# Five plain feature groups instead of six ahead of the block products, and more token tiles transposed by DMA

## The chip, the cores and the metric

The kernel runs on one core of a Trainium2 chip. The metric is the device time of one execution in microseconds (us); three executions of the kernel before gave a median of 938.21 us (937.78 to 938.38).

## What is computed

Two kinds of layer alternate, A, B, A, B, each added to its input after a layer norm over the 1024 features of each of 2048 tokens. Layer A is a spectral filter; layer B, which the change touches, is a two-matrix network with the Mish activation. Everything is bf16 at the borders.

```
def _A_ref(x, w_r, w_i):                       # x: 1 x 2048 x 1024
    X = rfft2(x.astype(float32), axes=(-2, -1))
    return irfft2(X * (w_r + 1j * w_i), s=(2048, 1024)).astype(bfloat16)

def _B_ref(x, w1, b1, w2):                     # w1: 1024 x 3584, w2: 3584 x 1024
    h = x @ w1 + b1
    sp = log1p(exp(-abs(h))) + where(h > 0, h, 0)
    return (h * tanh(sp)) @ w2

x = A_x
x = x + _A_ref(_layernorm(x), A_w_r, A_w_i)
x = x + _B_ref(_layernorm(x), B_w1, B_b1, B_w2)
x = x + _A_ref(_layernorm(x), A_w_r, A_w_i)
x = x + _B_ref(_layernorm(x), B_w1, B_b1, B_w2)
```

## The kernel before, in words

**Order.** The program is written out by hand: every call adds an instruction to the in-order program of one engine (PE, DVE, ACT, POOL, or SP, which only issues DMAs), and the waits follow from the buffers that the instruction reads and writes. So the order of the Python calls is the order on each engine, and an instruction that waits holds up everything behind it on its engine. SBUF is one arena that is handed out by offset (`alloc`); a buffer inherits the waits of whatever lay there before.

**Tokens and features in layer B** (`layer_B`, L1085; it is called twice, the second time with `last=True`). The 2048 tokens are 16 tiles of 128, and 4 tiles make a chunk, so chunks 0 and 1 are the first half (tiles 0 to 7), chunks 2 and 3 the second. The 3584 features are 14 groups (`fg`) of 256. A tile is normalised on DVE (`apply`, L517) and then transposed into the chunk's buffer `XT[c]`. There are two ways: `transposed` (L1100) does 8 transposes on PE (L1109) and copies the PSUM bank out on DVE or ACT (L1114); `turned` (L1119) prepares 8 DMA transposes of 128x128 on SP's queue, which `turn(n)` (L1130) issues n at a time. `normal(j)` (L1461) is `apply` followed by `turned`.

**First half, first matrix.** The first groups are computed plainly by `mm1` (L1134): per chunk and group two outputs of 8 matmuls each, 512 tokens wide, or 256 wide where only half of the chunk is there yet; the Mish runs on ACT (L1152). Weights come into `w1_buf`, which layer A fills at its end (L950). Calls given as `mid` come between the two outputs. The remaining groups go through `quads` (L1178): one group for both chunks together, as a Strassen-like product with 7 block products of 4 matmuls (28 in all, L1186) where the plain way takes 32. It needs sums of the weight blocks and of the token blocks (`token_sums`, L1156). An iteration n of `quads` has this order on PE: A11 and S2 of group n, then A22 and S4 of group n-1, then S1, A12 and S3 of group n. After S4 of group n-1 the function `after(n-1)` is called, which places the work of other engines.

**Weight slots.** A slot of 7168 bytes a partition holds 4096 bytes of raw weights and three sums. `fill_slot` (L1071) works in two ways. The first time a group is met, in the first layer B, SP loads the raw weights (512 KB), POOL makes four sums (L1081), and POOL's queue stores the slot to a scratch tensor (896 KB). Afterwards SP loads the finished slot (896 KB) from scratch. Each block product waits for the whole slot, sums included (L1188). There are four slots WE0 to WE3 and three slots WS0 to WS2, which lie where `w1_buf` lay. In the kernel before, `quads` runs groups 6 to 13: seven have a slot of their own, and group 13 refills WE0 in `after(0)`, to be used in iteration 7.

**Second matrix and second half.** `products` (L1276) multiplies the activations of the first half by the second matrix in 7 stages of 4 token tiles, 14 matmuls each (L1268). `extra(n, t)` (L1535) is called after every one of these 28 steps: it calls `turn(2)`, so that the transposes still waiting go out two a step. At step (1, 3) it makes the scales of tiles 12 to 15, hands tile 12 to the DMA transposes and normalises 13, 14 and 15, which PE transposes at step (2, 2); ACT copies these out. Then `quads` runs all 14 groups for the second half, and `products` ends the layer. There the three slots WS0 to WS2 are used in turn, each refilled in `after(n)` for group n+3.

The lines that the steps of the prediction touch, as they stand before:

```
        mm1(0, 4)
        at_tiles(1)
        mm1(0, 5, mid=turns(1, 0, 1))
...
            if n > 3:
                normal(4 + n)
                turn(4)
...
                    reads=[s.res, s.rs] + list(res), writes=[self.r_bank[bank]])
```

`turns(1, 0, 1)` are the PE transposes of tiles 4 and 5; `stats_dve`, `scales` and `apply` for these two tiles come on DVE after the residual additions of tiles 4 to 7 (L1396).

Of the kernel before, what the change touches and what calls it, by code (L numbers as in the profile page):

```python
# [180 lines left out]
class KB:  # L181
# [513 lines left out]
    def layer_A(self, li):  # L695
# [6 lines left out]
        o, K = self.o, 1024  # L702
# [244 lines left out]
        self.residual_first()  # L947
        if li == 0:
            self.op(self.pool, lambda e: e.tensor_copy(self.B1[:], self.B1h[:]), reads=[self.r_b1h], writes=[self.r_b1])
        self.w1_buf = [self.alloc(f"W1_{i}", (self.ob["WS"] + i * 4096, 140 * K)[i > 4], [8, 256]) for i in range(6)]  # L950
        for fg in range(6):
            self.load_w1(self.w1_buf[fg].ap, fg, [self.w1_buf[fg].res], after=self.r_ut)

    @staticmethod
# [130 lines left out]
    def layer_B(self, li, last):  # L1085
# [7 lines left out]
        def open_xt(c):  # L1093
            off = self.ob[f"XT{c}"]
            XT[c] = self.alloc(f"XT{c}", off, [8, 512])
            r_xt[c] = self.sub_res(XT[c], f"xt{c}h", 2, off, 8192)
            for r in r_xt[c]:
                r.begin()

        def transposed(c, t, xn, eng=None, bank=None):  # L1100
            if bank is None:
                bank = 6 + nt[0] % 2
                nt[0] += 1
            xn.unread = False
            if t == 0:
                open_xt(c)
            fns = []
            for db in range(8):
                fns.append(lambda e, db=db: e.transpose(PSb[:, bank, db * P:(db + 1) * P], xn.ap[:, db * P:(db + 1) * P],  # L1109
                                                        self.IDENT[:]))  # L1110
            self.group(fns, reads=[xn.res, self.r_ident], writes=[self.r_bank[bank]])
            dst = XT[c].ap[:, :, t * P:(t + 1) * P]
            src = PSb[:, bank, :].rearrange("p (a b) -> p a b", b=P)
            fn = (lambda e: e.activation(dst, src, ACT.Copy)) if eng is act else (lambda e: e.tensor_copy(dst, src))  # L1114
            self.op(eng or dve, fn, reads=[self.r_bank[bank]], parts=[r_xt[c][t // 2]])
# [3 lines left out]
        def turned(c, t, xn):  # L1119

            x, r = XT[c], r_xt[c][t // 2]
            for db in range(8):
                def one(db=db):
                    self.dma(sp, x.ap[:, db, t * P:(t + 1) * P], xn.ap[:, db * P:(db + 1) * P], f"xt{c}_{t}", reads=[xn.res],
                             parts=[r], transpose=True)
                    if db == 7:
                        xn.unread = False
                turning.append(one)
# [5 lines left out]
        def mm1(c, fg, half=None, mid=()):  # L1134
            wb = self.w1_buf[fg]
            x = XT[c]
            tok = slice(0, 512) if half is None else slice(256 * half, 256 * half + 256)
            w = tok.stop - tok.start
            for fl in range(2):
                if fl:  # L1140
                    for f in mid:
                        f()
                ft = 2 * fg + fl
                bank = nh[0] % 3
                nh[0] += 1
                fns = []
                for db in range(8):
                    fns.append(lambda e, db=db, bank=bank, fl=fl: e.matmul(  # L1148
                        PS[:, bank, 0:w], wb.ap[:, db, fl * P:(fl + 1) * P], x.ap[:, db, tok], start=(db == 0), stop=(db == 7)))
                self.group(fns, reads=[wb.res] + (r_xt[c] if half is None else [r_xt[c][half]]), writes=[self.r_bank[bank]])  # L1150
                at, ra = at_of(c, ft), r_at[c % 2][ft]
                self.op(act, lambda e, bank=bank, ft=ft, at=at: e.activation(at[:, tok], PS[:, bank, 0:w], ACT.Mish,  # L1152
                                                                      bias=self.B1[:, ft:ft + 1]),
                        reads=[self.r_bank[bank], self.r_b1], writes=[ra])
# [99 lines left out]
        def load_b(stages, n, k):  # L1254
            PB[n][k] = load_w2(stages[n][1], k, f"R{(2 * n + k + 1) % 4}")
# [122 lines left out]
        def at_tiles(c):  # L1378
            r_at[c] = [None] * NF
            for k in range(2):  # L1380
                off = self.ob["A"] + 14336 * (2 * k + c)
                AT[c][k] = b = self.alloc(f"AT{c}{k}", off, [NF // 2, 512])
                for i in range(NF // 2):
                    r = r_at[c][2 * i + k] = Res(f"AT{c}_{2 * i + k}")
                    r.inherit(b.res)
                    self.live.append((off + i * 1024, off + i * 1024 + 1024, r))
# [12 lines left out]
        def turns(c, *ts):  # L1399
            return [lambda t=t: transposed(c, t, xn[4 * c + t]) for t in ts]  # L1400
# [40 lines left out]
        for fg in range(1, 4):  # L1441
            mm1(0, fg, 1)
            if fg > 1:
                self.stats_act(4 + fg)
        mm1(0, 4)
        at_tiles(1)
        mm1(0, 5, mid=turns(1, 0, 1))
        self.sums_to_mv(6, 2)
        self.scales(6, 2)
        for j in (6, 7):  # L1450
# [1 line left out]
        gate = Res("gate")  # L1452
        gate.set_w(dve, dve.count)
        early = self.open_slots("WE", self.ob["W2"], 0, 1, 2, 3)
        for n in range(4):
            self.fill_slot(early[n], 6 + n, [gate])
        for fg in range(2):
            mm1(1, fg, 0, mid=turns(1, 2, 3) if fg else ())
        for fg in range(2):
            mm1(1, fg, 1)  # L1460
        def normal(j):  # L1461
            if j % 4 == 0:
                open_xt(j // 4)
            turned(j // 4, j % 4, self.apply(j))

        ws = []
        for fg in range(2, 6):
            if fg in (2, 4, 5):
                ws += self.open_slots("WS", self.ob["WS"], len(ws))
                self.fill_slot(ws[-1], 9 + len(ws))  # L1470
            mm1(1, fg)
            if fg == 2:
                token_sums(0, last=False)
            if fg == 3:
                for j in range(8, 12):
                    residual(j)
        order = early + ws + early[:1]
        B = token_sums(0)
        self.xn_buf = self.xn_out + [self.alloc(f"XN{i}", self.ob["XN2"] + i * 2048, [self.D]) for i in range(2)]

        def after(n):
            if n == 0:
                self.fill_slot(order[7], 13)
            if 1 <= n < 4:
                load_b(STD, n // 3, (n - 1) % 2)
            if n < 4:
                self.stats_dve(8 + n)
            if n == 4:
                self.scales(8, 4)
            if n > 3:  # L1490
                normal(4 + n)
                turn(4)
            for j in ((), (), (), (), (), (12, 13), (14,), (15,))[n]:
                residual(j)
        quads(list(range(6, 14)), order, B, after, lead)
        self.junk = self.alloc("JUNK2", self.ob["JUNK2"], [self.D])
        self.xn_buf = [self.alloc(f"XN{i}", self.ob["XN12"] + i * 2048, [self.D]) for i in range(2)] + self.xn_out
        w2 = {}
        if not last:
            for name, k, slot, prog in (("B21", 1, "R0", sp), ("B12", 0, "Q1", sp), ("B22", 0, "Q3", pool), ("B12", 1, "Q2", pool),  # L1500
                                        ("B22", 1, "Q4", sp)):
                w2[slot] = load_w2(name, k, slot, prog)
            PB[1][1] = w2["R0"]
        else:
            load_b(STD, 1, 1)
            self.fill_slot(ws[2], 2)
# [28 lines left out]
        def extra(n, t):  # L1535
            if n == 0:
                self.stats_act(12 + t)
            if not last:
                own_sums(n, t)
            if (n, t) == (1, 3):  # L1540
                self.sums_to_mv(12, 4)
                self.scales(12, 4)
                normal(12)
                for j in (13, 14, 15):
                    xn[j] = self.apply(j)
            if (n, t) == (2, 2):
                for j in (13, 14, 15):
                    transposed(3, j - 12, xn[j], act, (6, 7, 0)[j - 13])
            turn(2)
            if (n, t) == (4, 3) and not last:  # L1550
                ws[2:] = self.open_slots("WS", self.ob["WS"], 2)
                self.fill_slot(ws[2], 2)
            if n == 6 and not last:
                self.stats_act(t)
            if (n, t) == (5, 3):
                ws[0:2] = self.open_slots("WS", self.ob["WS"], 0, 1)
                for i in range(2):
                    self.fill_slot(ws[i], i)
                token_sums(1, last=False)
            if (n, t) == (6, 1):  # L1560
                B.update(token_sums(1))
        products(0, self.ob["WS"], STD, extra, last)
        order = [ws[n % 3] for n in range(14)]
# [85 lines left out]
```

## Time and profile before

| what | value |
|---|---|
| median of three executions | 938.21 us (937.78 to 938.38) |
| the profiled execution | 936.66 us |
| its span, first to last instruction | 934.9 us |
| PE busy | 875.9 us (94%) |
| DVE busy | 619.1 us (66%) |
| ACT busy | 427.5 us (46%) |
| POOL busy | 159.0 us (17%) |
| mean granted PE clock | 0.987 |

Times in the profile are from the start of the span. The first layer B begins near 113 us and its first `quads` at 172.05 us; the second layer B has its first `quads` at 628.43 us. Matmuls are pipelined, so the duration that is printed for one (379 ns for 512 columns) is longer than the distance to the next; the distance is read from a run of them in the chain of waits (216 matmuls in 46.62 us are 0.2158 us each).

### The profile page before, as it was taken

Reading aid. Unit: us, or ns where it says so; the run is one execution under the profiler, and the core shown is the slowest. Engines: PE = TensorE matmul, PEld = TensorE weight load, DVE = VectorE, ACT = ScalarE, POOL = GpSimd, SP = SyncE. Lnnn points to the kernel's source line nnn. Section 1 sums busy time; section 2 is a strip of 40 time slices with the busy share of each in tenths; the row PEclk is TensorE's granted clock in tenths of the full one; section 3 lists DMA queues with packets and bytes.
Section 4 is the critical chain, followed back from the end, with each engine's and each line's share of the span. In section 5 each row is a group of like instructions: output and inputs, shape, how many; then the busy total and the mean of one; then the engine's idle time right before and its main releaser. Section 6 shows DMA issues by size and latency. Waiting matters only on the chain.

```text
span 934.9 us, 13481 instructions
## 1 busy us (share of the span) xinstructions
PE 875.9 (94%) x5473; PEld 471.7 (50%) x5473; DVE 619.1 (66%) x973; ACT 427.5 (46%) x623; POOL 159.0 (17%) x183
## 2 busy tenths in 40 slices
PE   0799799999999999999979987999999999999998
PEld 0577486444444444444437765754444444444443
DVE  7698468686889667568746865647746665554473
ACT  7798485456203485510008975745551015552000
POOL 4922004950005642000130200000000000000000
PEclk9999999999999999999999997999999999999999
DMA  9969854676895488274640797433255635832432
GB/s 288 265 227 300 204 151 131 216 249 171 268 274 196 164 314 296 91 261 142 241 133 32 227 228 196 158 118 119 54 190 175 207 113 193 279 118 78 171 127 110
DMA packets 146335, 174.68 MB, mean 187 GB/s; under 512 B 66248, under 2 KB 125736, under 8 KB 146152
## 3 DMA queue, kind: packets, MB, share of 16 engines
q1 hardware_dynamic: 133424, 127.48, 44.5%
q0 software_dynamic: 10672, 44.67, 13.4%
q10 hardware_dynamic: 2176, 1.66, 0.6%
q8 instruction: 43, 0.70, 0.3%
q14 instruction: 20, 0.16, 0.0%
HBM read 130.00 MB, written 40.89 MB: 183 GB/s over the span
## 4 chain that ended last, share of the span: by engine, by line
PE 83%; DMA 5%; DVE 5%; ACT 2%; SPq 2%; POOL 1%; issue 1%; DVEq 0%; ACTq 0%; POOLq 0%
PE PS L1268 35%; PE PS L1186 28%; PE PS L1148 9%; SPq L251 2%; PE PS L799 2%; PE PS L725 2%; PE PS L824 2%; PE PS L1020 2%; POOL ARENA L1081 1%; PE PS L1109 1%; DMA ARENA<-in_A_x_dram 1%; DMA ARENA<-c_bt 1%; DMA ARENA<-u_scratch 1%; DMA u_scratch<-ARENA 1%; PE PS L635 1%; ACT ARENA L641 1%
## 5 line engine op out<-in xcount | busy, mean ns | idle before, releaser
L1268 PE MATMUL PS<-ARENA 128*128 128x512 bf16 x1568 | 340.1, 379 | 0.0
L1186 PE MATMUL PS<-ARENA 128*128 128x512 f16 (+1 forms) x1232 | 267.8, 379 | 0.4 <-POOL ARENA L1081 0.3
L1268 PEld LDWEIGHTS PS<-ARENA 128*128 128x128 bf16 x1568 | 153.4, 98 | 184.5
L1191 DVE TENSOR_TENSOR ARENA<-PS,ARENA 128x512 f32<-128x512 f32 x220 | 151.7, 691 | 95.7 <-PE PS L1186 90.7
L1186 PEld LDWEIGHTS PS<-ARENA 128*128 128x128 bf16 x1232 | 120.1, 98 | 146.8 <-POOL ARENA L1081 2.2
L1196 ACT ACTIVATE ARENA<-ARENA,B 128x512 bf16<-128x512 f32 x132 | 95.1, 721 | 66.5 <-DVE ARENA L1191 60.6
L574 ACT ACTIVATE ARENA<-PS 128x512 f32<-128x512 f32 (+2 forms) x82 | 61.1, 745 | 119.1 <-PE PS L1186 96.4
L1148 PE MATMUL PS<-ARENA 128*128 128x256 bf16 (+1 forms) x576 | 86.7, 308 | 0.3
L1081 POOL TENSOR_TENSOR ARENA<-ARENA 128x512 bf16<-128x512 bf16 x56 | 71.4, 1274 | 72.6 <-DVE ARENA L524 58.3
L453 ACT ACTIVATE ARENA<-XS 128x1024 bf16<-128x1024 bf16 x52 | 54.8, 1053 | 36.5 <-DVE XS L1319 33.0
L1148 PEld LDWEIGHTS PS<-ARENA 128*128 128x128 bf16 x576 | 55.2, 98 | 26.7 <-DVE ARENA L1114 1.0
L1293 DVE TENSOR_TENSOR ARENA<-ARENA 128x3584 bf16<-128x3584 bf16 x32 | 63.9, 2018 | 0.0
L1319 DVE TENSOR_TENSOR XS<-PS,ARENA 128x512 bf16<-128x512 f32 x52 | 35.7, 690 | 38.9 <-PE PS L1268 38.7
L1152 ACT ACTIVATE ARENA<-PS,B 128x256 bf16<-128x256 f32 (+1 forms) x72 | 38.3, 542 | 35.3 <-PE PS L1148 34.8
L1311 DVE TENSOR_TENSOR ARENA<-PS,ARENA 128x512 f32<-128x512 f32 x48 | 32.9, 688 | 28.9 <-PE PS L1268 28.4
L1196 ACT ACTIVATE ARENA<-PS,B 128x512 bf16<-128x512 f32 x44 | 30.2, 686 | 18.0 <-PE PS L1186 18.0
L1307 DVE TENSOR_TENSOR ARENA<-ARENA,XS 128x512 f32<-128x512 f32 x52 | 36.7, 731 | 0.5
L1163 DVE TENSOR_TENSOR ARENA<-ARENA 128x2048 f16<-128x2048 bf16 x16 | 25.3, 1582 | 17.6 <-PE PS L1148 17.3
L799 PE MATMUL PS<-ARENA 128*128 128x256 bf16 x256 | 32.4, 273 | 3.9 <-DVE ARENA L788 3.2
L472 DVE BATCH_NORM_STATS2 BN<-XS 128x6 f32<-128x512 bf16 x52 | 32.6, 669 | 4.5 <-DMA XS<-in_A_x_dram 4.5
L444 ACT ACTIVATE RS<-MV,EPS 128x1 f32<-128x1 f32 (+2 forms) x11 | 3.3, 296 | 70.7 <-DVE MV L565 70.0
L777 ACT ACTIVATE ARENA<-PS 128x1024 bf16<-128x1024 f32 x32 | 33.3, 1071 | 4.5 <-PE PS L773 4.5
(97 smaller groups left out, 820.9 us busy)
## 6 DMA issues: line engine op xcount, KB each, us to landing
ARENA<-in_B_w_dram SPq DMA_DIRECT2D x30, 896.0 KB, 6.4
ARENA<-w1s_scratch SPq DMA_DIRECT2D x30, 896.0 KB, 4.7
ARENA<-w2s_scratch SPq DMA_DIRECT2D x24, 896.0 KB, 6.7
ARENA<-in_B_w_dram SPq DMA_DIRECT2D x26, 512.0 KB, 5.2
w1s_scratch<-ARENA POOLq DMA_DIRECT2D x14, 896.0 KB, 4.2
u_scratch<-ARENA SPq DMA_DIRECT2D x14, 512.0 KB, 3.5
ARENA<-u_scratch SPq DMA_DIRECT2D x14, 512.0 KB, 5.9
w2s_scratch<-ARENA POOLq DMA_DIRECT2D x8, 896.0 KB, 4.1
```

What stands on the lines that cost most here:

```text
L453: self.op(act, lambda e, i=i, f=f: e.activation(junk.ap, x, f, accum_out=sums[:, i:i + 1]), reads=[self.r_xs[j]], writes=[junk.res], parts ...
L574: fn = (lambda e: e.activation(dst, src, ACT.Copy)) if scale is None else \
L799: fns.append(lambda e, c=c, part=part: e.matmul(ps[:, c * 256:(c + 1) * 256], yk.ap[:, part, c * P:(c + 1) * P], t[:, (128, 0)[part]:(384, ...
L1081: self.op(self.pool, lambda e, dst=A(dst), x=A(x), y=A(y), op=op: e.tensor_tensor(dst, x, y, op), reads=[b.res] + list(after), writes=[b.rs])
L1148: fns.append(lambda e, db=db, bank=bank, fl=fl: e.matmul(PS[:, bank, 0:w], wb.ap[:, db, fl * P:(fl + 1) * P], x.ap[:, db, tok], start=(db ...
L1152: self.op(act, lambda e, bank=bank, ft=ft, at=at: e.activation(at[:, tok], PS[:, bank, 0:w], ACT.Mish, bias=self.B1[:, ft:ft + 1]), reads= ...
L1186: self.group([lambda e, db=db: e.matmul(PS[:, bank, :], A[:, db, :], mov[:, db, :], start=(start and db == 0), stop=(db == 3), skip_group_ ...
L1191: self.op(dve, lambda e: e.tensor_tensor(dst.ap, PS[:, bank, :], x.ap, ALU.add), reads=[self.r_bank[bank], x.res], writes=[dst.res])
L1196: self.op(act, lambda e: e.activation(at, src, ACT.Mish, bias=self.B1[:, ft:ft + 1]), reads=[res, self.r_b1], writes=[ra])
L1268: self.group([lambda e, i=i, k=k, b=PB[n][k].ap: e.matmul(PS[:, bank, :], ap[:, i, t * P:(t + 1) * P], b[:, i - 7 * k, :], start=(start an ...
L1293: self.op(dve, lambda e: e.tensor_tensor(ap[dst][:, f, :], ap[x][:, f, :], ap[y][:, f, :], op), reads=part(x, k) + part(y, k), writes=part ...
L1307: self.op(dve, lambda e: e.tensor_tensor(a[t], a[t], x, ALU.add), reads=[rx], writes=[r[t]])
```

## The change

In both layers B, `w1_buf` has five buffers and loads instead of six, and group 5 moves from the plain part to `quads`, which now runs nine groups (5 to 13). The PE transposes of tiles 4 and 5 move from the middle of `mm1(0, 5)` to the middle of `mm1(0, 4)`. Chunk 1 has three groups in halves and two whole instead of two and four, and the transposes of tiles 6 and 7 come in the third group instead of the second. The seven first groups of `quads` (5 to 11) have a slot of their own; groups 12 and 13 refill WS0 and WS1, in `after(4)` and `after(5)`, behind the `turn(4)` of the same call. `turn(4)` is called five times instead of four. At step (1, 3) of the first `products`, tiles 12 and 13 (in the last layer 12, 13 and 14) are handed to the DMA transposes, so that PE transposes two tiles (in the last layer one) at step (2, 2) instead of three.

```diff
-        self.w1_buf = [self.alloc(f"W1_{i}", (self.ob["WS"] + i * 4096, 140 * K)[i > 4], [8, 256]) for i in range(6)]
-        for fg in range(6):
+        self.w1_buf = [self.alloc(f"W1_{i}", self.ob["WS"] + i * 4096, [8, 256]) for i in range(5)]
+        for fg in range(5):
             self.load_w1(self.w1_buf[fg].ap, fg, [self.w1_buf[fg].res], after=self.r_ut)
...
-        mm1(0, 4)
         at_tiles(1)
-        mm1(0, 5, mid=turns(1, 0, 1))
+        mm1(0, 4, mid=turns(1, 0, 1))
...
-            self.fill_slot(early[n], 6 + n, [gate])
-        for fg in range(2):
-            mm1(1, fg, 0, mid=turns(1, 2, 3) if fg else ())
-        for fg in range(2):
+            self.fill_slot(early[n], 5 + n, [gate])
+        for fg in range(3):
+            mm1(1, fg, 0, mid=turns(1, 2, 3) if fg == 2 else ())
+        for fg in range(3):
             mm1(1, fg, 1)
...
-        for fg in range(2, 6):
-            if fg in (2, 4, 5):
-                ws += self.open_slots("WS", self.ob["WS"], len(ws))
-                self.fill_slot(ws[-1], 9 + len(ws))
+        for fg in (3, 4, 5):
+            ws += self.open_slots("WS", self.ob["WS"], len(ws))
+            self.fill_slot(ws[-1], 8 + len(ws))
+            if fg == 5:
+                break
             mm1(1, fg)
...
-        order = early + ws + early[:1]
+        order = early + ws + ws[:2]
...
-            if n == 0:
-                self.fill_slot(order[7], 13)
...
+            if 3 < n < 8:
+                normal(4 + n)
             if n > 3:
-                normal(4 + n)
                 turn(4)
-            for j in ((), (), (), (), (), (12, 13), (14,), (15,))[n]:
+            if n in (4, 5):
+                self.fill_slot(order[n + 3], n + 8)
+            for j in {5: (12, 13), 6: (14,), 7: (15,)}.get(n, ()):
                 residual(j)
-        quads(list(range(6, 14)), order, B, after, lead)
+        quads(list(range(5, 14)), order, B, after, lead)
...
+        by_pe = 15 if last else 14
...
-                normal(12)
-                for j in (13, 14, 15):
+                for j in range(12, by_pe):
+                    normal(j)
+                for j in range(by_pe, 16):
                     xn[j] = self.apply(j)
             if (n, t) == (2, 2):
-                for j in (13, 14, 15):
+                for j in range(by_pe, 16):
                     transposed(3, j - 12, xn[j], act, (6, 7, 0)[j - 13])
```

More of the change, by code (lines that the diff above doesn't have):

```diff
@@ L1466, in layer_B @@
         ws = []
-        for fg in range(2, 6):
-            if fg in (2, 4, 5):
-                ws += self.open_slots("WS", self.ob["WS"], len(ws))
-                self.fill_slot(ws[-1], 9 + len(ws))
+        for fg in (3, 4, 5):
[3 more added lines that the diff above has]
+                break
             mm1(1, fg)
-            if fg == 2:
+            if fg == 3:
                 token_sums(0, last=False)
-            if fg == 3:
+            else:
                 for j in range(8, 12):
                     residual(j)
-        order = early + ws + early[:1]
+        order = early + ws + ws[:2]
         B = token_sums(0)
```

## The prediction

> **What bounds the kernel now.** I began with the page's busy times and its chain that ended last, by engine, then listed that chain in order of time.
>
> ```profile
> PE 875.9 (94%) x5473; PEld 471.7 (50%) x5473; DVE 619.1 (66%) x973; ACT 427.5 (46%) x623; POOL 159.0 (17%) x183
> ...
> PE 83%; DMA 5%; DVE 5%; ACT 2%; SPq 2%; POOL 1%; issue 1%; DVEq 0%; ACTq 0%; POOLq 0%
> ```
>
> ```profile
> 137.08 10.42 PE PS L1148 x72
> 147.50 0.89 PE PS L1109 x16
> 148.39 4.35 PE PS L1148 x32
> 153.22 1.30 DVE ARENA L1114 x2
> 154.57 17.48 PE PS L1148 x96
> 172.05 46.62 PE PS L1186 x216
> 218.67 3.02 PE PS L1268 x14
> 221.69 1.73 PE PS L1186 x8
> 223.42 30.22 PE PS L1268 x140
> 253.64 1.34 PE PS L1109 x24
> ```
>
> From 137 to 255 us PE runs almost without a gap: a 512-wide matmul every 46.62/216 = 0.2158 us, a 256-wide one every 0.109. So PE sets the end here, and PE work removed is time gained only while data stay ahead of PE. The second layer B has the same pieces 456.38 us later. What stays ahead, and by how much, is read from the timelines of DVE, SP and POOL:
>
> ```profile
> 138.59 2.50 DVE L1396 TENSOR_TENSOR XS<-XS,ARENA 128x1024 bf16<-128x1024 bf16 x4 [3.06 <-ACT ARENA L574]
> ...
> 145.54 1.00 DVE L524 TENSOR_SCALAR ARENA<-XS,MV,RS 128x1024 bf16<-128x1024 bf16 x2
> 147.98 1.29 DVE L1114 COPY ARENA<-PS 128x1024 bf16<-128x1024 bf16 x2 [1.45 <-PE PS L1109]
> ```
>
> ```profile
> 206.80 6.31 SPq L250 DMA_TRANSPOSE ARENA<-FD  x5
> ```
>
> ```profile
> 318.37 4.85 POOL L1081 TENSOR_TENSOR ARENA<-ARENA 128x512 bf16<-128x512 bf16 x4 [6.57 <-DMA ARENA<-in_B_w_dram]
> 323.52 0.57 POOL L251 DMA_DIRECT2D w1s_scratch<-ARENA  x1 [0.30 <-POOL ARENA L1081]
> 324.53 4.85 POOL L1081 TENSOR_TENSOR ARENA<-ARENA 128x512 bf16<-128x512 bf16 x4 [0.44 <-DMA ARENA<-in_B_w_dram]
> ```
>
> The first shows tiles 4 and 5 normalised at 146.5 us, by a DVE chain that starts when ACT finishes a copy at 138.5; PE asks for them at 147.5, so 1 us is in hand. The second: a DMA transpose holds SP for 1.26 us. The third: a refill of a slot in the later quads, where nothing stands before it on SP; the four sums take 4.85 us.
>
> **What the Trainium skill says.** "DMA: Bandwidth & Descriptors", section "Issuing engines are not separate DMA queues", calls the time a sequencer needs to initiate a DMA "usually small relative to the DMA itself". The trace disagrees for transposes: 1.23 us of SP at the median, against 0.43 for a plain weight load. Its section "SWDGE vs HWDGE vs iDMA" lets only SP or ACT issue transposes; the trace has all 80 on SP. "VectorE: DVE Perf Modes", section "The three transpose paths", gives 1309 ns for a 128x128 DMA transpose, near that 1.23, and 390 ns on PE, where this trace shows 0.89 us for 16, or 56 ns each, which I use. "TensorE: Matmul & The Clock Gate", Part 1, says that PE falls to half clock after an idle window of about 3.4 us and needs about as long to recover. The trace agrees: after a 6.48 us wait, at 488.19 us, 48 matmuls of 128 columns took 5.29 us, 110 ns each where 56 is usual.
>
> **The change, part by part** (first layer unless said).
>
> *Group 5 into quads.* 32 wide matmuls become 28: 4 x 0.2158 = 0.86 us less PE in each layer, 1.73 in all. The extra five DVE additions (0.69 each) and four or so ACT passes (0.7) lie beside 6.04 us of PE per iteration, as for the other eight: nothing.
>
> *Fewer tiles on PE.* 24 transposes take 1.34 us, so a tile is 0.447: one less and then two less, -1.34 in all. Their DMAs, 8 and 16 more, go out two a step: 2.5 us of SP in a step of 14 x 0.2158 = 3.02 us, with output stores (0.34) and loads (0.43) between. They are due only at the token sums of stage 5; nothing. ACT loses three copies that waited on nothing.
>
> *Tiles 4 and 5 asked for earlier.* PE now reaches their transposes after 48 half-width and only 8 wide matmuls: 137.08 + 48 x 0.109 + 8 x 0.2158 = 144.05. The DVE chain doesn't move, since its releaser, the ACT copy, comes before the removed work. Tile 4 is ready near 146.1, so PE waits 2.1 us; tile 5 follows 0.5 later and fits. The second layer has the same chain: 593.46 + 6.97 = 600.4 against 602.5. Together **+4.2**. Bounds: 0 (if DVE reached it 2 us sooner) to 2.5 a layer. The chunk then ends at 148.8 (150.12 before), chunk 1 takes 3.46 less, and quads start at 167.3 instead of 172.05. The transposes of tiles 6 and 7 come a group later in chunk 1, with tile 7 done near 151.2 and PE there at 153.2: no new wait.
>
> *First fills.* POOL's sums start when tile 7 is normalised, 1.3 us earlier, and came every 6.1 us (152.45 to 201.4 for eight). Fill n is ready near 157.7 + 6.1n, needed at 167.3 + 6.04n or earlier by 1.7: covered by 8 us. One W1 load less at the start was not waited for: nothing.
>
> *The refill of WS0.* This is the large term; I use the old times, since all shift alike. Iteration 0 has 20 matmuls (4.32 us), the others 28 (6.04). Iteration 5 starts at 172.05 + 4.32 + 4 x 6.04 = 200.5, S4 of group 4 ends 16 matmuls on, at 204.0, and WS0 is free. Iteration 7 needs it at 212.6: 8.6 us in hand. The refill stands on SP behind `turn(4)`, whose transposes wait for DVE's scales and tile 8 (done at 206.77). They start at 206.80, and the fifth would begin at 211.85; the refill takes its place, 7.9 us after the slot came free. A raw load in the third view lands 3.7 us after issue (median of the DMA view from 310 to 332 us): 215.6; add 0.3 for the transposes still in the rings. Sums 4.85, waits between 0.1: ready at 220.8. Needed at 212.6: PE waits **8.2 us**. Up to 1.5 more if the load takes its overall median of 5.2, up to 1.6 more if a transpose holds SP for 1.66 (14 in 23.31 us at 229.06). Behind the refill on SP stand four transposes, then the refill of WS1, issued 5.5 us later; it is on POOL by the time the first sums end and done 5.5 us after them, before iteration 8 asks 6.04 later: no more wait. On POOL the store and the later w2 loads stand behind these sums; iterations 7 and 8, now 8 us late, cover them.
>
> In the last layer there are no sums. SP is at its transposes at 663.17 (16 in 20.97 us, 1.31 each), so the refill goes at 668.4. A load of the same 896 KB, issued at 684.19 right behind transposes, landed in 4.9 us; so 673.3, needed at 628.43 + 4.32 + 6 x 6.04 = 669.0: PE waits **4.3 us** (3.9 to 6.1 with landings of 4.5 to 6.7).
>
> *The clock after the waits.* Idle for 8.2 us PE goes cold; at 488 us that lost 48 x (110 - 56) ns = 2.6. I take 2.0 in the first layer (0 to 2.6). 4.3 us covers an idle window only now and then: 0.7 in the last (0 to 2.6).
>
> *w2 loads.* They stand on SP behind four more transposes and two refills, yet SP ends those near 61 us into quads, while PE, with its wait, needs 63: no delay.
>
> **Sum.** First layer: -0.86 - 0.45 + 2.1 + 8.2 + 2.0 = +11.0. Last: -0.86 - 0.89 + 2.1 + 4.3 + 0.7 = +5.3. Together +16.3, on the profiled execution's 936.66 (span 934.9 and 1.8 around it) 953.0. That execution lies 1.55 below the median of 938.21; on the median it is **954.5 us**, which I forecast.
>
> **The rivals.** The measurement can tell about 0.2%, 1.9 us, from no change.
>
> *The refill is in time.* Were SP to reach it as soon as WS0 is free, it would take 3.9 (in the third view S4 ends near 311.00 + 16 x 0.2158 = 314.45, the sums start at 318.37) + 4.85 + 0.1 = 8.9 of 8.6 us, a wait of 0.3, and none in the last layer. Then -3.07 + 4.2 + 0.3 = +1.4: 939.6. For it: that pace is what the later quads show. Against: SP's queue is in order, and the plain loads at 227.28 came out only behind the sixteenth transpose.
>
> *Faster.* The saved 3.07 us come through because DVE is ahead of PE at both places: it finishes tiles 4 and 5 by 144.1, and tile 8 early enough for SP to be past its four transposes when WS0 comes free. It decides from tile 8 being ready by 198.9, 7.9 us earlier than now; then 938.21 - 3.07 + 0.3 = 935.4. Against: tile 8's scales stand behind S4 of group 4 on DVE, so it cannot be ready before 204.
>
> *Waits that grow.* Transposes and loads slow each other: 1.66 us a transpose (+1.6, +1.4), loads at 5.2 and 6.7 (+1.5, +1.8), clock lost in full (+0.6, +1.9): +25.1, 963.3. For it: SP's plain DMAs land after 1.7 to 11.4 us. Against: DMAs are only about a tenth busy where the last layer's turns run (655 to 690).
>
> **How the numbers follow.** Forecast 0.68, in its own range of 948 to 960 (unknown costs at their ends, not all at once); refill in time 0.10; faster 0.05; growing waits 0.17. With 947 to 964 the two rivals below (0.15) and a tail of the last are left out. Faster by over 0.2%: 0.05; within: 0.07 (most of the second case); slower: 0.88.
>
> **What would show it.** Right: the profile after has a PE idle before L1186 of some 8 us, released by POOL's L1081, at the eighth group of the first quads, one of some 4 us released by a DMA from the scratch tensor in the last layer, and two of 2 us before L1109, released by DVE L524; SP issues the refill directly after four transposes. Wrong: L1186 runs on through both quads, or the refill leaves SP before the transposes; or PE clock stays full after the 8 us.

## The result, and the profile after

The changed kernel takes **960.08 us** (median of six, 958.27 to 963.24) against 937.86 for the kernel before in the same runs (936.83 to 938.38): a ratio of 1.0243, 95% interval 1.0222 to 1.0264, slower by 22.2 us. The forecast was 954.5 with a range of 947 to 964. The profiled execution took 958.89 us, its span is 957.1 (before: 936.66 and 934.9).

The same views, now of the kernel after. First the page's busy times and its chain by engine:

```profile
PE 872.2 (91%) x5398; PEld 473.9 (50%) x5473; DVE 626.6 (65%) x983; ACT 426.7 (45%) x626; POOL 159.2 (17%) x183
...
PE 76%; DVE 7%; DMA 7%; ACT 3%; SPq 3%; POOL 2%; issue 1%; ACTq 0%; DVEq 0%; POOLq 0%
```

PE's busy time is 3.7 us shorter (75 of its 5473 matmuls have no record in this trace), and its share of the chain has gone from 83% to 76%. What took its place stands in the chain in order of time (start, duration, what):

```profile
149.46 1.07 PE PS L1109 x16
...
171.56 4.49 PE PS L1186 x20
...
207.75 1.21 SPq L250
209.00 1.23 SPq L250
210.28 1.24 SPq L250
211.56 4.19 DMA ARENA<-in_B_w_dram
215.89 1.15 POOL ARENA L1081
...
220.77 10.26 PE PS L1186 x40
231.08 3.40 PE PS L1186 x15
234.49 3.02 PE PS L1268 x14
...
679.20 4.97 DMA ARENA<-w1s_scratch
684.21 10.49 PE PS L1186 x40
```

Before, L1186 ran through from 172.05. Now the chain leaves PE: SP issues transposes, then the refill of WS0 at 211.56, the load lands, POOL makes its sums, and PE goes on at 220.77. In the last layer the same, without POOL. PE's waits over the whole span (releaser, total, times, longest):

```profile
PE PS L1186 <- POOL ARENA L1081: 9.4, 3, 8.5
...
PE PS L1109 <- DVE ARENA L524: 4.5, 4, 2.1
PE PS L1186 <- DMA ARENA<-w1s_scratch: 4.2, 1, 4.2
...
PE PS L1186 <- ACT ARENA L1152: 1.6, 2, 0.8
```

The last row, 0.78 us before the first block product of each layer, was in no step of the prediction. After the two long waits PE is cold, that is, the clock granted to it is down to half (the columns that matter are the stretch, PE's busy time with its matmuls, and the granted clock, third from the end):

```profile
220.00:224.00 4.00, 3.23 (x9) 1.19 (x10) 0.00 (x0) 1.21 (x2) 3.44 (x4) 0.53 0.80 281
684.00:688.00 4.00, 3.79 (x10) 1.42 (x11) 0.46 (x1) 1.21 (x2) 0.00 (x0) 0.57 0.50 152
```

Cut where PE passes from one line to the next, the two profiles give this account. "Forecast" is the sum of the prediction's terms for that stretch.

| stretch (us) | before | after | forecast | measured |
|---|---|---|---|---|
| start to first PE transposes of layer B | 119.8 | 123.1 | 0 | +3.2 |
| plain groups, first B | 52.07 | 48.50 | -4.8 | -3.6 |
| first quads, first B | 46.62 | 62.76 | +16.2 | +16.1 |
| second matrix, first half | 87.67 | 87.23 | -0.45 | -0.4 |
| from there to the transposes of the last B | 269.7 | 269.3 | 0 | -0.4 |
| plain groups, last B | 52.35 | 48.44 | -4.8 | -3.9 |
| first quads, last B | 46.62 | 58.71 | +11.0 | +12.1 |
| second matrix, first half | 87.68 | 86.78 | -0.9 | -0.9 |
| the rest | 172.3 | 172.3 | 0 | 0 |

### The profile page after: what moved, and what is told of

Same layout as the page of the kernel before. It is cut to its first block, busy times and chain, and to the rows that moved or that the text cites. A ratio compares the mean times of both kernels' runs of the same rounds, so it can differ in the third digit from the quotient of the medians.

```text
span 957.1 us, 13444 instructions
## 1 busy us (share of the span) xinstructions
PE 872.2 (91%) x5398; PEld 473.9 (50%) x5473; DVE 626.6 (65%) x983; ACT 426.7 (45%) x626; POOL 159.2 (17%) x183
## 4 chain that ended last, share of the span: by engine, by line
PE 76%; DVE 7%; DMA 7%; ACT 3%; SPq 3%; POOL 2%; issue 1%; ACTq 0%; DVEq 0%; POOLq 0%
PE PS L1268 34%; PE PS L1186 25%; PE PS L1148 6%; POOL ARENA L1081 2%; SPq L251 2%; PE PS L799 2%; PE PS L725 2%; PE PS L824 2%; PE PS L1020 2%; DMA ARENA<-in_B_w_dram 1%; PE PS L1109 1%; DMA ARENA<-c_bt 1%; DMA ARENA<-u_scratch 1%; DMA ARENA<-in_A_x_dram 1%; SPq L250 1%
## 5 line engine op out<-in xcount | busy, mean ns | idle before, releaser
L1186 PE MATMUL PS<-ARENA 128*128 128x512 f16 (+1 forms) x1264 | 281.7, 382 | 16.4 <-POOL ARENA L1081 9.4
L1191 DVE TENSOR_TENSOR ARENA<-PS,ARENA 128x512 f32<-128x512 f32 x230 | 158.5, 691 | 117.1 <-PE PS L1186 113.0
L1186 PEld LDWEIGHTS PS<-ARENA 128*128 128x128 bf16 x1288 | 126.3, 98 | 170.8 <-POOL ARENA L1081 10.0
L1196 ACT ACTIVATE ARENA<-ARENA,B 128x512 bf16<-128x512 f32 x138 | 99.2, 721 | 71.4 <-DVE ARENA L1191 65.1
L1148 PE MATMUL PS<-ARENA 128*128 128x256 bf16 (+1 forms) x540 | 72.7, 291 | 0.6
L1311 DVE TENSOR_TENSOR ARENA<-PS,ARENA 128x512 f32<-128x512 f32 x48 | 33.0, 688 | 30.4 <-PE PS L1268 30.0
L1152 ACT ACTIVATE ARENA<-PS,B 128x256 bf16<-128x256 f32 (+1 forms) x68 | 34.2, 509 | 30.5 <-PE PS L1148 30.2
L781 DVE TENSOR_TENSOR ARENA<-ARENA 128x1024 bf16<-128x1024 bf16 x32 | 22.0, 688 | 21.0 <-ACT ARENA L777 21.0
```

Source lines behind the costliest of these rows:

```text
L1148: fns.append(lambda e, db=db, bank=bank, fl=fl: e.matmul(PS[:, bank, 0:w], wb.ap[:, db, fl * P:(fl + 1) * P], x.ap[:, db, tok], start=(db ...
L1186: self.group([lambda e, db=db: e.matmul(PS[:, bank, :], A[:, db, :], mov[:, db, :], start=(start and db == 0), stop=(db == 3), skip_group_ ...
L1191: self.op(dve, lambda e: e.tensor_tensor(dst.ap, PS[:, bank, :], x.ap, ALU.add), reads=[self.r_bank[bank], x.res], writes=[dst.res])
L1196: self.op(act, lambda e: e.activation(at, src, ACT.Mish, bias=self.B1[:, ft:ft + 1]), reads=[res, self.r_b1], writes=[ra])
```

## The experiments

The theory: the refills of WS0 and WS1 are late because they stand on SP behind DMA transposes, PE's cold clock adds to that, and tiles 4 and 5 are asked for before DVE has them. The rivals: the load or POOL is the limit; the DMAs of the extra transposes cost something; the waits are taken up elsewhere. All times below are medians; the ratios are against the kernel before in the same runs, with the 95% interval, and are not worked out from the medians, so they can differ from those by 0.1%. Where a stretch is quoted, it is from the one profiled execution of a run.

**The refill ahead of the transposes** (on the changed kernel).

```diff
+            if n in (4, 5):
+                self.fill_slot(order[n + 3], n + 8)
             if 3 < n < 8:
                 normal(4 + n)
             if n > 3:
                 turn(4)
-            if n in (4, 5):
-                self.fill_slot(order[n + 3], n + 8)
```

> The changed kernel with one thing moved: in after(4) and after(5) the refill of WS0 and WS1 is placed ahead of the normalisation and the four DMA transposes of the same call. If the refill's place on SP's queue made the waits: in the first layer SP issues the first refill as S4 of group 4 ends, the wait before the eighth group falls from 8.5 us to 0.3; the second refill still stands behind the four transposes of after(4), some 1.5 us late, so about 1.8 us before the ninth group; in the last layer both waits (4.2) go, and with them the cold PE (1.9 and 2.1 us). About -14.5 us against the changed kernel, 945 to 946. If the load or POOL itself is the limit and SP's queue is not: the wait stays above 6 us in the first layer and the time above 955.

Measured: 947.43 us, 1.0095 (1.0082 to 1.0108), 12.7 us less than the changed kernel. SP and PE of this run:

```profile
199.19 6.41 SPq L251 DMA_DIRECT2D ARENA<-in_B_w_dram  x2
208.00 5.03 SPq L250 DMA_TRANSPOSE ARENA<-FD  x4
213.13 0.53 SPq L251 DMA_DIRECT2D ARENA<-in_B_w_dram  x1
```

```profile
215.38 6.22 PE L1186 MATMUL PS<-ARENA 128*128 128x512 bf16 x28 [1.55 <-POOL ARENA L1081]
222.87 6.22 PE L1186 MATMUL PS<-ARENA 128*128 128x512 bf16 x28 [1.28 <-POOL ARENA L1081]
```

The wait of 8.5 us became 1.55; the second refill, still behind four transposes, has a wait of 1.28. The last layer's wait is gone: its quads take 52.68 us, which is 52.66 without any wait (46.62 and one more group). The refill's place on SP was the cause of most of the wait; the load and POOL's sums ask for 1.2 us more than the 0.3 that I gave them. The two quads together are 13.0 us shorter than in the changed kernel, where the expectation had 14.5, which fits the fall of 12.7. In this profile the plain groups of the first layer took 51.20 us, in the changed kernel 48.50: 1.0 of that lies before the transposes of tiles 4 and 5, where PE came into the layer with a low clock, and 1.7 after them, which the next runs explain.

**PE kept at work through the refill waits** (on the changed kernel).

```diff
+                    if N == 9 and n == 7:
+                        self.spin(18 if last else 36, 7)
                     product(n, a, "A11", "B11", True)
```

> The changed kernel with matmuls that nobody reads (36 in the first layer, 18 in the last, 7.8 and 3.9 us of PE, into PSUM bank 7) just before the product that waits for the refill of WS0. If the 55 matmuls after the waits are slow because PE went cold: the waits end at the same times, the stretch from there to the second matrix takes 11.9 us in both layers instead of 13.7 and 13.9, and the time falls by 3.9 us to 956. If they are slow for another reason (POOL, DVE or the loads taking SBUF): the stretch stays at 13.7 and 13.9 and the time is unchanged.

Measured: 958.18 us, 1.0193 (1.0175 to 1.0212), 1.9 less. Its granted clock, and the stretch after the first wait:

```profile
220.00:224.00 4.00, 3.07 (x15) 1.36 (x15) 0.57 (x1) 1.21 (x2) 3.35 (x5) 1.00 0.78 257
687.00:691.00 4.00, 3.95 (x20) 1.81 (x19) 2.52 (x5) 2.34 (x4) 0.00 (x0) 1.00 0.74 240
```

```profile
212.85 7.93 PE L652 MATMUL PS<-BD 128*128 128x512 bf16 x36
221.71 12.03 PE L1186 MATMUL PS<-ARENA 128*128 128x512 bf16 x54 [0.93 <-POOL ARENA L1081]
```

The clock stays at 1.00. From the end of the wait to the second matrix it is 233.58 - 221.71 = 11.87 us instead of 234.32 - 220.77 = 13.55, and 12.1 instead of 13.8 in the last layer: 1.7 us in each is the cold clock, shown. The time was expected to fall by 3.9 us and fell by 1.9, which the executions (956.74 to 959.18 against 958.27 to 963.24) hardly separate from nothing. In the profile the waits also ended 0.2 and 0.8 us later, counted from the start of the quads, and the plain groups took 50.72 and 50.55 us, 2 more than in the profile of the changed kernel.

**The transposes of tiles 4 and 5 one group earlier, alone** (on the kernel before).

```diff
-        mm1(0, 4)
         at_tiles(1)
-        mm1(0, 5, mid=turns(1, 0, 1))
+        mm1(0, 4, mid=turns(1, 0, 1))
+        mm1(0, 5)
```

> The kernel before with one thing moved: the PE transposes of tiles 4 and 5 come in the middle of group 4 instead of group 5; six plain groups, eight block groups. If the DVE chain to tiles 4 and 5 ends at a fixed time: PE waits 2.1 us before them in each layer and nothing later takes it up, +4.2 us, 942.1. If the wait is absorbed later (tiles 6 and 7 or the first quads were waiting anyway): under +1.

Measured: 942.09 us, 1.0058 (1.0035 to 1.0081), as forecast; but the executions lie between 940.37 and 948.35. In the profile, an execution of 948.35, both waits are there, and after both PE is cold. The trace records the clock in steps of 3.41 us; here is the step with the first wait (146.85 to 148.94 us) and the next:

```profile
146.32:149.73 3.41, 1.32 (x17) 0.82 (x16) 2.80 (x13) 3.27 (x7) 0.00 (x0) 1.00 0.71 214
149.73:153.14 3.41, 3.41 (x14) 1.44 (x11) 3.03 (x14) 0.00 (x0) 0.00 (x0) 0.50 0.00 0
```

The plain groups took 56.6 and 56.5 us instead of 52.07 and 52.35: 2.1 us of wait, and 2.0 to 2.4 that the forecast had not counted, most of it cold PE. So a wait of 2.1 us can cost nearly twice its length. In the profile of the changed kernel the same wait (147.38 to 149.46) lies across the end of a step, and the clock stays:

```profile
145.24:148.65 3.41, 2.08 (x11) 0.90 (x10) 3.08 (x12) 3.35 (x9) 0.00 (x0) 1.00 0.99 294
148.65:152.06 3.41, 2.60 (x24) 1.70 (x25) 3.00 (x9) 1.50 (x3) 0.00 (x0) 1.00 0.03 8
```

This pattern holds in all the profiles of this document. From the transposes of tiles 4 and 5 to the end of the first half's second matrix, in both layers B, each of the 15 steps that held 2.03 us or more of a PE wait was followed by a step at half clock, and no step that held 1.80 or less was. It was read from the traces afterwards; no run moves a wait against the steps.

**More tiles turned by DMA, alone** (on the kernel before).

```diff
-                normal(12)
-                for j in (13, 14, 15):
+                for j in range(12, by_pe):       # by_pe: 14, in the last layer 15
+                    normal(j)
+                for j in range(by_pe, 16):
                     xn[j] = self.apply(j)
...
-                for j in (13, 14, 15):
+                for j in range(by_pe, 16):
                     transposed(3, j - 12, xn[j], act, (6, 7, 0)[j - 13])
```

> The kernel before with one thing changed: one more tile in the first layer and two more in the last go by DMA transposes instead of PE. If their DMAs are hidden: three times 0.447 us of PE, -1.3 us, 936.5. If SP's queue, which has to issue 8 and 16 more, delays the loads of the second matrix: PE waits before a stage of the products, no gain or slower than before.

Measured: 942.11 us, 1.0035 (1.0023 to 1.0047): slower by 4.1 (938.00 for the kernel before in the same runs), the second theory. The second matrix's first half takes 92.57 us instead of 87.67, and 88.47 instead of 87.68. PE's longest wait there, and SP:

```profile
285.54 26.01 PE L1268 MATMUL PS<-ARENA 128*128 128x512 bf16 x112 [3.51 <-DVE ARENA L1260]
```

```profile
280.59 1.12 SPq L251 DMA_DIRECT2D ARENA<-in_B_w_dram  x2
```

In the kernel before, SP issued these two loads 11 us earlier (they are the first two of the three):

```profile
269.35 16.61 SPq L251 DMA_DIRECT2D ARENA<-in_B_w_dram  x3
```

The two loads that SP issues here at 280.59 are for the sixth stage; the eight further transposes hold SP for 10 us before them. The first of the two landed at 285.41 (279.09 in the kernel before), and PE goes on at 285.54. The view names a DVE sum (L1260) as the releaser, since that ended at 285.42; but the sum is of a later stage's matrix, so the load is what PE needed. In the changed kernel the same transposes cost nothing (87.23 and 86.78 us). The likely reason, not tested by itself, is the fifth call of `turn(4)` in one more iteration of quads; the waits are not needed for it, as the next run but one shows (87.47 and 86.78 us without them).

**Another PSUM bank at the start** (on the changed kernel).

```diff
-        nt, nh, no = [0], [0], [0]
+        nt, nh, no = [0], [2], [0]
```

> The changed kernel with the plain groups starting their PSUM banks at 2 instead of 0, so that their last output no longer lies in the bank that the first block product writes. If the 0.78 us that PE stands before the quads of both layers is a wait for that bank's Mish: both waits go, -1.6 us, and the SP and POOL waits of the refills stay as they are (8.5 and 4.2). If it is a wait for something else that ends at the same time (the token sums on DVE, the slot): the 0.78 us stays, with another releaser, and the time is unchanged.

Measured: 959.68 us, 1.023 (1.0215 to 1.0245), 0.4 less than the changed kernel, which its spread does not separate from nothing. In the profile the wait for ACT's L1152 before the first block product is gone in both layers; in the first:

```profile
170.42 2.75 PE L1186 MATMUL PS<-ARENA 128*128 128x512 bf16 x12
```

The plain groups of the last layer take 47.59 us instead of 48.44. Nothing of that reached the end of the layer: the refill's wait grew from 4.2 to 4.6 us, more of PE's work after it ran at half clock, and the quads took 59.70 instead of 58.71. In the first layer (refill wait 8.4) PE was cold after tiles 4 and 5 (clock 0.74 from 146 to 150 us), and the plain groups took 49.62. The wait is what it looked like: the plain groups now have 34 outputs over three banks, so the last one lies in bank 0, which the first block product writes.

**The refills in other slots** (on the changed kernel, with the bank shift).

```diff
-        order = early + ws + ws[:2]
+        order = early + ws + early[:1] + ws[:1]
...
+            if n in (0, 4):
+                self.fill_slot(order[7 + n // 4], 12 + n // 4)
             if 3 < n < 8:
                 normal(4 + n)
             if n > 3:
                 turn(4)
-            if n in (4, 5):
-                self.fill_slot(order[n + 3], n + 8)
```

> The changed kernel with group 12 refilling WE0 in after(0), group 13 refilling WS0 in after(4) ahead of its transposes, and the bank shift of the earlier run. All waits at the refills and at the first block product go. What is left of the change is the saved PE work, -3.1 us, and the wait before tiles 4 and 5, 2.1 to 2.3 us in each layer, in some executions with 1.6 to 2.9 us of cold PE behind it. Theory: 939 to 942. Rival: without the waits PE runs ahead of SP's transposes, and the loads of the second matrix come late as in the run that only turned more tiles; then the products take 3 to 5 us more in the first layer, 943 to 947.

Measured: 944.47 us, 1.0056 (1.0037 to 1.0074), but from 938.69 to 949.25. The quads take 52.67 us in both layers, no refill is waited for any more, and the second matrix keeps its pace (87.47 and 86.78), against the rival. The median is 2.5 to 5.5 above the theory, with the widest spread of all.

**Tiles 4 and 5 brought forward with POOL's help** (as the last run; the additions of tiles 6 and 7 on POOL, the transposes inside the second output of group 4).

```diff
-        for j in range(4, 8):
+        for j in (6, 7):
+            residual(j, pool)
+        for j in (4, 5):
             residual(j)
...
-        mm1(0, 4, mid=turns(1, 0, 1))
+        mm1(0, 4, mid=turns(1, 0, 1), cut=4)
```

> As the run with the other slots, and the tiles 4 and 5 brought forward: the residual additions of tiles 6 and 7 go to POOL, so that the DVE chain to tiles 4 and 5 is 1.25 us shorter, and their transposes stand 4 matmuls (0.86 us) later, inside the second output of group 4. If the wait is the chain as read: it falls from 2.1 us to under 0.3 in each layer, no cold PE, 936 if the products keep their pace; 939 to 941 if SP delays the second matrix in the first layer. If POOL's additions are slow and hold up tiles 6 and 7: a new wait of 1 to 3 us there.

Measured: 943.66 us, 1.0041 (1.0025 to 1.0058). The wait is 1.8 us, not 0.3. DVE and POOL of this run show where it went:

```profile
142.36 3.21 DVE L1401 TENSOR_TENSOR XS<-XS,ARENA 128x1024 bf16<-128x1024 bf16 x2 [3.06 <-ACT ARENA L574]
```

```profile
142.40 5.15 POOL L1401 TENSOR_TENSOR XS<-XS,ARENA 128x1024 bf16<-128x1024 bf16 x2 [45.42 <-ACT ARENA L574]
```

Beside POOL, two additions on DVE take 3.21 us, where four took 2.50: tiles 4 and 5 came 0.7 us later, and what stands behind them became 0.6 us shorter, so nothing was gained. The expectation's premise was wrong.

> As all_mended, but tiles 13, 14 and 15 are transposed on PE as before the change, in both layers. Theory of the SP queue: 8 and 16 transposes less on SP, so the products of both layers take the time of before (87.67 us from the first to the quads of the second half), 1.34 us more PE than all_mended needs but no late load; 936 to 937.5, and below all_mended if SP is what holds the products. If SP has room, it is 1.3 us slower than all_mended.

The same with tiles 13 to 15 on PE (`by_pe = 13`): 942.26 us, 1.0036 (1.0022 to 1.0049). Its second matrix takes 87.88 and 87.67 us against 87.66 and 86.78; the medians do not separate the two, and 936 to 937.5 was missed. What SP still costs the products after nine iterations of quads is little: in the first layer PE waits 0.3 us for a load with the tiles on SP, 0.8 in the next run.

**PE kept at work before tiles 4 and 5** (on the run with the other slots).

```diff
-        mm1(0, 4, mid=turns(1, 0, 1))
+        mm1(0, 4, mid=[lambda: self.spin(9, 5)] + turns(1, 0, 1))
```

> The run other_slots with 9 matmuls that nobody reads (1.9 us, PSUM bank 5) put just before the transposes of tiles 4 and 5, where PE waits 2.1 us. If what spread other_slots from 938.7 to 949.3 is PE going cold after that wait in some executions: the executions lie within 3 us of each other and the median falls from 944.5 to 939.5 to 941, with the wait itself still lost. If the spread comes from elsewhere (the DMAs of the first layer A): median and spread stay, 943 to 946.

Measured: 941.21 us, 1.0035 (1.0021 to 1.0048), and 940.52 to 942.94. That is 3.2 us above the kernel before in the same runs, where the run without these matmuls was 5.9 above. In the profile PE waits 0.15 us instead of 2.09 and its clock stays at 1.00; the time of the wait itself is still lost (the plain groups take 47.60 us in both layers). So cold PE was part of the median and of the spread of 10.6 us, but it is not shown to be all of the spread: five executions lie within 2.4 us here, and 13 within 5.9 in the next run, which keeps PE at work likewise; the kernel before lay within 5.0 in 24.

> As tiles_warm, with the transposes of tiles 4 and 5 four matmuls (0.86 us) later, inside the second output of group 4, and 5 unread matmuls before them. If the wait is for a fixed time on DVE: it falls from 2.1 to 1.25 us in each layer, 1.7 us less in all than tiles_warm, 938 to 939.5, level with the kernel before. If tile 5 or the copies to SBUF then end last: no gain over tiles_warm.

With 5 such matmuls and the transposes 4 matmuls later (`cut=4`): 939.7 us, 1.0025 (1.0013 to 1.0038). The plain groups take 46.30 and 47.46 us, but the layers differ only before the wait: from the transposes of tiles 4 and 5 to the quads it is 20.53 us in both, 0.63 less than in the last run, and those transposes come no later. So 1.3 of the expected 1.7 us came.

This is the best version tried, and it is still 1.7 us slower than the kernel before. Its profile says where that goes. In each layer the plain groups, from the transposes of tiles 2 and 3 on, are 5.2 us shorter (what is left of the wait is in them), and the quads are 6.04 longer by their ninth group: +0.8 twice. The first quads lose another 0.8, and the second matrix is 0.9 shorter in the last layer; together +1.6. In these quads PE waits 0.63 us for DVE. The cause is best seen in two other runs: two of DVE's additions of 128x1024 stand there, and they take longer when they fall beside POOL's sums for the refilled slot. In the run with PE kept at work (first line) POOL was at these sums from 206.50 to 211.92 us, in the run with the other slots (second line) only from 211.43:

```profile
209.26 3.21 DVE L1396 TENSOR_TENSOR XS<-XS,ARENA 128x1024 bf16<-128x1024 bf16 x2
209.70 1.28 DVE L1396 TENSOR_TENSOR XS<-XS,ARENA 128x1024 bf16<-128x1024 bf16 x2
```

In the first of these runs PE then waits 0.65 us for DVE, in the second not at all.

## Why the prediction was right, and where its sizes were off

**The direction and the mechanism were right.** The large term, the refill behind `turn(4)`, was put at 8.2 and 4.3 us; the waits were 8.5 and 4.2, SP issued the refill straight after the fourth transpose, and ahead of the transposes only 1.55 of the 8.5 us were left and nothing of the 4.2. The first term of the chain, the load, was 4.2 us to landing against 3.7 and 0.3.

**Group 5 into quads and the tiles on PE:** the quads grew by one group of 6.04 us, a plain group less took 3.46 twice, and the second matrix became 0.44 and 0.90 us shorter, as the sum has it. "Nothing" for the further DMA transposes held, but its cover is narrow: on the kernel before the same step costs 4.1 us in all. I had compared SP's time with PE's step by step, and not what SP had still queued when the steps began.

**Tiles 4 and 5:** 2.08 and 2.10 us of wait against 2.1. The step left out what such a wait does to the clock. The profile of the changed kernel shows none of it, but in the six profiles that have waits of 2.1 us here, the clock fell after 7 of 12; in two others it fell after none of four waits of 1.78 us. Of the ten stretches between the transposes of tiles 4 and 5 and those of tiles 6 and 7 that have the same instructions, five took 7.0 us and five 8.6 to 8.7: a fall costs 1.6 to 1.7 us. Which it was went with the place of the wait in the steps of the clock. The changed kernel's executions lie within 5.0 us, six of the kernel before within 1.6; but 24 of the kernel before in later runs lie within 5.0 as well, so the spread alone shows nothing.

**The clock after the refills:** 2.0 in the first layer was measured as 1.7, and the 0.7 of the last layer was too small: also 1.7, both against the run that kept PE at work. I had argued that a wait of 4.3 us seldom covers an idle window of 3.4 us, as the Trainium skill's "TensorE: Matmul & The Clock Gate", Part 1, describes it. In these traces 2.03 us of waiting within one step of 3.41 were enough. A wait of 4.18 us puts at least 2.09 us into one step wherever it lies, so by that reading (an estimate) it is always followed by half clock.

**The term that was missing** is the PSUM bank. The step "a plain group less" counted matmuls, and not that 34 outputs instead of 36 shift the bank that the last one uses: 0.78 us of waiting in each layer. Without it the last layer's stretch from the transposes of tiles 4 and 5 to the quads took 21.16 us instead of 22.10, so it is 0.94 us of time in each, 1.9 in all, shown by the bank shift.

**What the sum came to:** in the two layers B the profile has +19.4 us where the sum has +16.3. The bank (1.9) and the last layer's clock (1.0) make up nearly all of the difference. A further 3.2 us of the profile lie before the first layer B (0.4 comes back in the layer A between), where the program differs only in one W1 load less and in where the W1 buffers lie. There the profiles of kernels with six W1 loads reached layer B at 119.8, 120.1 and 122.0 us, those with five at 120.8 to 123.3; whether that is the change or chance stays open. The median grew by the same 22.2 us. Cold starts after tiles 4 and 5, which this profile lacks, would add about 2.0 us to the 19.4 (1.7 after 7 of 12 waits, in two layers: an estimate from other runs' profiles), which leaves 0.8 of the median open. So the range held the result, but the forecast was 5.6 us short of it for want of terms that the sum did not have.

**The rivals:** "in time" and "faster" fell with the first profile. "Waits that grow" (963.3) came nearer to the time than the forecast did, but by luck: transposes held SP for 1.23 us, loads landed as the forecast had it, and the clock cost 1.7 us each time, not the full 2.6. What was said against it misread a view: in the kernel before, DMAs are a tenth busy only from 663 to 684 us (0.11), where the transposes run alone, and 0.30 busy over the whole of 655 to 690.

## What to carry to other kernels

An engine's queue is part of the price of everything behind it: a refill that PE waited 1.55 us for in one place cost a wait of 8.5 us four transposes later, so when work is put on a queue, look up who stands behind it and when that one is needed. Removing busy work from the bottleneck engine also removes cover and shifts rotations (buffers, banks): go through every deadline that the removed work hid, and through the index of every ring it moved. And price a wait on PE with what follows it: here waits of 2.1 to 8.5 us were in most cases followed by about 1.7 us lost to a lower clock.

## What was not expected of the hardware

PE's clock fell to half for 3.41 us after waits as short as 2.1 us, after 7 of 12 of them: when all or nearly all of the wait (2.03 us or more) lay within one step of the clock's record, and not when the end of a step cut it into pieces of 1.80 us or less. Matmuls without use, put into the wait, kept it at 1.00. A tensor addition of 128x1024 bf16 took 0.63 us on DVE alone and 1.6 us while POOL did additions beside it.
